# Gated linear attention and a spatial gating unit on one core: three tokens to a partition, chunks of 96 tokens in small TensorE tiles, y made transposed

## The chip, the core and the metric

The kernel runs on one core of one Trainium2 chip. The metric is the device time in microseconds of one execution; lower is better. The core has five engines with queues of their own, each in order: TensorE (PE), VectorE (DVE), ScalarE (ACT), GpSimd (POOL) and SyncE (SP), which here only issues transfers. TensorE reads SBUF and writes PSUM, which has eight banks of 512 float32 for each of 128 partitions.

## The reference

```python
def _attn_ref(q, k, v, alpha):           # each 4 x 8 x 768 x 48 (batch, head, token, d)
    state = zeros((B, H, D, D)); y = zeros_like(q)
    for t in range(S):
        state = alpha[:, :, t, :, None] * state + einsum('bhd,bhe->bhde', k[:, :, t], v[:, :, t])
        y[:, :, t] = einsum('bhd,bhde->bhe', q[:, :, t], state)
    return y

x = attn_out.transpose(0, 2, 1, 3).reshape(B, S, H * D)      # 4 x 768 x 384
h = maximum(x @ w_in, 0)                                      # w_in 384 x 1024
u, v = h[..., :512], h[..., 512:]
v_n = (v - mean(v)) / sqrt(var(v) + 1e-6)                     # over the last axis
v_s = einsum('ts,bsd->btd', w_spatial, v_n) + b_spatial[None, :, None]   # w_spatial 768 x 768
out = (u * v_s) @ w_out                                       # w_out 512 x 384
```

Inputs and output are float32; inside, matmul operands are bfloat16.

## The kernel before, in words

The recurrence is computed in chunks. In a chunk, the logarithms of alpha (`la`) are summed along the tokens by a matmul with a triangle of ones (`cum`); `kt` is k times exp(-cum), `qt` is q times exp(cum). The scores are kt against qt, masked to the lower triangle (`ptm`), and y is the masked scores times v (`vb`) plus q times the state at the chunk's start (`sbd`). The state is carried from chunk to chunk: `z` adds the chunk's kt times v to it (the matmuls `upd`), `S` multiplies it by the chunk's total decay (`bc`), and `sb` copies it as bfloat16 into a block-diagonal tile.

The six chunks of 128 tokens of a batch come in two forms. `first(i)` treats one chunk with one token to a partition, its loads in pieces of 192 bytes. `pair(j)`, used for the first eight chunks (`PAIRS`), treats two chunks as 256 tokens, two tokens to a partition, in pieces of 384 bytes; its chunks are then 64 partitions each, so several matmuls run in tiles of 64 rows. Both transpose kt and qt by TensorE, evacuate them to `kqT`, and make y with tokens on the partitions. `finish_x` copies y to SBUF (`x_sb`), transposes it by TensorE and copies it again to `xT`, which has the 384 model columns on the partitions.

The second half works by batch: `second_v` (v, then its mean and variance, then `vn`), `second_u` (u, transposed), `second_s` (the spatial matmul with the transposed `w_spT`, plus bias, into `vsb`; then the product with u, `gT`) and `second_o` (times w_out, and a store). `weights` transposes w_spatial row block by row block.

The order of everything is written out by hand in the table `PLAN`. Every operation has a number; `P43` emits operation 43 on TensorE, `A`, `D`, `G`, `S`, `Q` on ACT, DVE, POOL, SP and as a transfer's end; numbers behind a colon add matmuls on a constant tile (`junk`) ahead of the next operation that takes a PSUM bank. So `PLAN` also says which engine does an operation that could run on several. Waits are put in by the framework from the tiles that operations read and write. PSUM banks are taken in turn. SP's queue holds the loads of q, k, v and alpha, those of the weights between them, and the stores.

Of the kernel before, what the change touches and what calls it, by code (L numbers as in the profile page):

```python
# [11 lines left out]
ALU = mybir.AluOpType  # L13

class Op:


    def __init__(self, key, eng, dur, emit, deps=(), prio=0.0, take=None, lat=0.13, cols=0):  # L20
        self.key = key
        self.eng = {eng: dur} if isinstance(eng, str) else dict(eng)
        self.emit, self.prio, self.lat, self.cols = emit, prio, lat, cols
        self.take = [take] if isinstance(take, Slot) else list(take or ())
        self.deps = [d for d in deps if d is not None]
        self.done = False
        self.big = False


class Ring:  # L30


    def __init__(self, bufs):
        self.bufs = bufs


class Slot:
    def __init__(self, ring):
        self.ring, self.users = ring, []


ENGINES = {
    "kt": {"POOL": 0.9},
    "vb": {"POOL": 0.48, "ACT": 0.42},
    "S": {"POOL": 0.5},
    "sb": {"POOL": 0.73, "DVE": 0.95},
    "vn": {"DVE": 0.42},
    "xe": {"ACT": 0.4},
    "ev": {"DVE": 0.34, "ACT": 0.48},
    "u": {"ACT": 0.39, "DVE": 0.49},  # L50
    "o": {"ACT": 0.4},
}
PAIRS = (0, 1, 2, 3)
ACT_STATS = ((2, 2), (1, 4))
LETTERS = {"P": "PE", "D": "DVE", "A": "ACT", "G": "POOL", "S": "SP", "Q": "DMA"}

PLAN = """
G32 S34 Q33 S36 G0 S38 S40 Q35 D1 Q37 S94 A42 D2 Q39 S96 P43:512:512:192 P53:64 A44 A45 G46 Q41 S98 A54 A55 D47 G56
D57 P51:512 Q95 P49 S100 P59:64 P61 A58 G48 D60 A50 D52 P63:192 Q97 S163 A62 P247 D65 A102 P71 D248 P74 D72 A64 Q99
S167 P103:96 G66 P113 D73 A104 A114 D68 D76 A115 Q101 P249 S165 G116 A105 A250 D117 G106 D107 P121:512 Q164 S169 D75  # L60
A122 P111:64 G67 P109 D112 P119 A110 G69 D120 Q168 S4 P131:192 D70 P134 G108 P77 G118 D133 G3 P123:128 A171 Q166
D132 S307 D125 A124 A78 P172 D136 P81 G126 P182 A173 Q170 S9 D135 P79 A183 D127 A82 P137 A174 Q5 D128 A184 S311 P142
D176 P138 G185 P83 A139 D175 A80 P140 A84 D186 P178 A143 P180 D179 A177 G187 P188 P190 Q308 S309 D189 G129 P144 P192
D181 A145 D191 A141 G6 D194 A193 A8 P197 D7 Q10 P200 G195 D199 P85 S14 A315 G196 D198 P157 A86 G130 D201 P316 A158
P146 D202 Q312 A317 D159 A318 P203 A147 P204 P208 D87 P88 A205 Q310 A209 G11 P206 D12 P326 A89 D13 P210 A207 D320
P151 S18 Q15 A211 D148 S313 P212 A327 S367 G319 A328 P324 D152 P223 A213 D330 G329 P215 A160 D90 A325 Q19 P334 S371
P322 A216 P221 D162 G16 A224 D217 P153 A222 P332 G17 A91 D323 P229 A335 P225 D92 Q314 S22 D231 A154 P149 D93 A333
G20 D214 P232 A226 P227 A150 Q368 D230 S369 P155 D234 A228 D161 A233 P235 D21 Q372 A218 S409 D237 P238 A236 D219
P344 G321 A156 Q23 D239 P255 S446 D220 G331 P259 D345 A375 P376 D346 P336 A377 A378 A380 P260 D338 Q370 S373 A240
D381 P256 A337 D261 A24 P263 G339 Q410 D257 S411 P264 D25 G379 P241 Q447 D341 P347 A242 S448 D265 P251 A243 G342  # L70
D349 Q374 P244 P383 G340 S413 A245 D246 P252 D348 A417 G262 P275 Q412 A385 S415 D253 P276 D384 G258 A382 Q449 P350
D277 A454 S450 P390 A351 G343 P267 D391 Q414 P418 S480 G278 D392 P354 P352 A419 P279 Q416 A353 S26 G421 P268 A355
P386 A420 A422 P356 D269 Q451 G266 P393 S482 A357 D387 P280 A394 D423 G388 P455 Q481 D281 S484 P395 A457 P425 A456
G389 P361 D427 A424 Q27 D397 G458 A396 S452 P358 D426 A459 A362 D460 P398 G254 A359 D363 P428 A399 P462 G270 P432
D429 A488 P271 D433 A463 G430 Q483 S577 P401 D464 P489 D434 A28 G31 P407 Q485 A490 G30 S486 D400 P272 A492 P435 A402
G491 Q453 D29 P405 S581 A436 D273 P283 G282 A408 D493 Q578 S579 P437 P469 A284 G274 D438 P495 A406 D470 P403 Q487
A496 S611 G461 D471 P287 A439 G431 A497 Q582 D404 P291 S583 A288 D360 P465 P498 Q580 A585 S648 P472 D466 A292 D500
P586 G494 A364 P440 Q612 G467 D499 A587 S690 P295 A473 G468 D366 A588 A590 Q584 S615 P474 A441 G589 P501 D475 D591
P299 Q649 A502 D442 S728 A476 P503 A296 P593 G592 P477 A619 Q691 D505 D504 S613 A300 D594 P517 D365 A478 Q616 P596
D595 S650 P506 A443 D597 A479 D518 P513 Q729 D445 S652 A507 P600 D444 P620 A508 D602 Q614 P519 S692 A621 P533 D509  # L80
A656 P303 Q651 S694 A514 D601 P515 A510 Q653 A622 P525 A698 D512 S617 D511 A624 P529 G623 D516 A520 Q693 P657 S654
P534 A304 D625 G598 A659 A658 P526 D535 Q695 G599 A661 S732 P699 D527 P530 A701 A700 G660 P545 Q618 A703 D531 S730
A736 P627 G536 P603 D629 Q655 P546 S762 A604 D704 G528 P537 A628 D662 Q733 P538 S696 D547 G626 P605 P664 D539 G702
A606 P634 Q731 A607 P630 S766 A665 P541 D631 G663 A666 D635 P737 Q763 G632 P542 S858 A738 D636 G548 A739 P671 A741
P706 Q697 D543 S892 P667 A708 G532 P608 D742 A707 D672 Q767 P521 S764 G740 A609 P637 D633 A770 P549 Q859 A638 S734
D668 P522 D673 P550 Q893 G705 D523 S862 P639 P744 D551 A640 P713 G524 A641 Q765 D746 P674 A745 S860 D714 P771 G669
A675 P642 D715 A772 Q735 G670 S768 A774 P751 P676 A643 P553 G540 D678 Q863 D677 A866 S864 D775 P709 P716 A554 G773
D752 P679 Q861 A717 S929 D753 A900 G544 P557 A680 D710 Q769 D610 S896 P777 G711 A558 P718 P867 A743 G712 Q865 P561
D719 A869 D779 S933 A868 D720 A681 P747 G552 D778 P686 Q930 D644 S894 P721 A871 G870 A562 P754 D748 Q897 A722 D872
S971 P565 G749 A755 D687 G750 A645 Q934 P780 P874 S931 A566 D782 P756 P569 G776 A757 A723 Q895 D781 G873 S975 P573  # L90
D876 A758 A875 P783 D724 Q972 S898 P682 A784 A570 P881 D646 Q932 P785 P759 S973 D787 A786 D883 A574 P788 A937 Q976
D882 S935 A760 P796 D683 A789 P684 Q899 D761 S1012 A797 P877 P800 A685 D790 Q974 A725 P901 S1008 P688 A903 A801 D647
P794 A979 Q936 D726 S1042 P938 A791 D727 P798 D878 A902 Q1013 D792 P810 A940 A905 S1046 D793 G904 P802 A939 D795
P980 Q1009 D906 G879 S1010 P803 A981 P811 G941 A799 D804 Q1043 A942 P806 S977 D689 A982 G805 A984 P807 D812 Q1047
P884 S571 D943 P822 G907 A885 D985 P823 G813 Q1011 D808 S1044 P908 P886 G983 P945 A910 D887 Q978 P814 D909 S1014
A888 D824 P911 A946 G809 P815 D912 Q572 A947 P889 S1048 D816 G944 A1016 Q1045 S575 D880 P987 A890 G817 P915 P952
A988 D916 Q1015 P1017 G913 P830 A1050 D989 A1019 G914 P834 A1018 D917 Q1049 A1021 P1051 D953 G825 P838 A1052 Q576
D954 A835 P948 G1020 P831 A1054 D949 P918 D832 G950 P818 A919 D1022 G986 P819 A839 D1055 G951 P920 P1024 D820 A921
P994 A1025 G1053 D922 P990 P826 D996 A1026 P955 G1023 D995 P827 G833 A956 D991 P1031 D828 P957 P1057 G992 A959 D1032
P923 A958 G821 A1059 D1033 P960 A924 G829 P997 A1058 D925 P967 A998 G993 P1027 A961 P999 P1060 D1028 A968 P842 D962  # L100
G1029 A1000 A1001 P963 G1030 A843 D1061 P1002 A1056 S844 D1062 A964 P1034 S305 A1003 D891 P850 S836 Q845 A1035 S840
P1063 D1004 Q306 P846 A1064 Q837 A926 P1065 P1036 A847 P965 D1067 Q841 D1037 A1038 D1066 P854 D928 D966 P1068 A851
D927 A1005 P969 A1069 D1006 P1074 D1007 P1039 D1070 P1078 A1040 P1080 A855 D1041 P1076 A970 S856 P1090 S297 D1075
A1071 P1094 S285 D1079 A1077 Q857 P1082 S289 D1072 P1106 Q298 D1073 S301 D1081 P1086 Q286 S567 P1087 Q290 S563 P1083
D1088 Q302 S852 P1095 G1089 Q568 P1091 S559 D1096 P1102 Q564 S293 D1092 G1097 P1098 D1084 Q853 S848 P1103 D1093 Q560
G1085 S555 P1099 D1104 Q294 P1107 D1105 P1113 Q849 D1100 Q556 P1117 A1114 D1108 G1101 P1110 D1109 S1115 A1118 P1111
S1119 P1121 D1112 Q1116 P1137 A1122 Q1120 P1125 D1138 S1123 P1133 S1139 A1126 P1129 D1134 Q1124 S1127 S1135 A1130
Q1140 S1131 Q1128 Q1136 Q1132
"""


def replay(ops, fill, plan):

    for word in plan.split():
        number, *junk = word[1:].split(":")
        op, eng = ops[int(number)], LETTERS[word[0]]
# [8 lines left out]
def kernel(  # L125
# [12 lines left out]
    nc = tc.nc  # L138
# [1009 lines left out]
```

## Time and profile before

| | |
|---|---|
| time, median of 3 runs | 145.1 us (144.96 to 145.82) |
| span of the profiled execution | 142.9 us; the page gives no time for what lies around it |
| PE, DVE, ACT, POOL busy | 132.9, 122.2, 108.2, 86.0 us |
| instructions | 4,962, of them 1,910 matmuls and 1,923 weight loads |
| moved by transfers | 28.64 MB in 89,000 packets |

The span runs from the first to the last instruction of the one profiled execution. A row of the page's groups has the line and engine, the operation, what it writes and reads, the count, then the busy time and the mean of one in ns, and the idle time before it with what ended it. In the rows by slices each digit is the busy share of a fortieth of the span, in tenths. A chain row is start, duration and what. Matmuls overlap, so their mean duration is not the time that one adds.

### The profile page before, as it was taken

Reading aid. Unit: us, or ns where it says so; the run is one execution under the profiler, and the core shown is the slowest. Engines: PE = TensorE matmul, PEld = TensorE weight load, DVE = VectorE, ACT = ScalarE, POOL = GpSimd, SP = SyncE. Lnnn points to the kernel's source line nnn. Section 1 sums busy time; section 2 is a strip of 40 time slices with the busy share of each in tenths; the row PEclk is TensorE's granted clock in tenths of the full one; section 3 lists DMA queues with packets and bytes.
Section 4 is the critical chain, followed back from the end, with each engine's and each line's share of the span. In section 5 each row is a group of like instructions: output and inputs, shape, how many; then the busy total and the mean of one; then the engine's idle time right before and its main releaser. Section 6 shows DMA issues by size and latency. Waiting matters only on the chain.

```text
span 142.9 us, 4962 instructions
## 1 busy us (share of the span) xinstructions
PE 132.9 (93%) x1910; PEld 83.7 (59%) x1923; DVE 122.2 (85%) x290; ACT 108.2 (76%) x280; POOL 86.0 (60%) x147
## 2 busy tenths in 40 slices
PE   7978977999799999999999999999999999999990
PEld 3464857456465666665655666656666666556460
DVE  6759998998989799989789999889889989776950
ACT  3567398899976799999987889999878688760131
POOL 6945853748317999971288879910999994003700
PEclk9999999999999999999999999999999999999999
DMA  4999989999998999999899999999999103229645
GB/s 115 268 261 265 250 201 327 334 322 328 251 224 163 213 276 161 203 176 198 145 205 192 164 209 162 208 143 206 187 156 222 55 7 137 86 98 338 229 150 180
DMA packets 89000, 28.64 MB, mean 200 GB/s; under 512 B 83728, under 2 KB 87440, under 8 KB 88976
## 3 DMA queue, kind: packets, MB, share of 16 engines
q1 hardware_dynamic: 88944, 28.32, 92.0%
q8 instruction: 15, 0.25, 0.8%
q14 instruction: 9, 0.07, 0.2%
q0 software_dynamic: 32, 0.00, 0.0%
HBM read 23.60 MB, written 4.72 MB: 198 GB/s over the span
## 4 chain that ended last, share of the span: by engine, by line
PE 70%; DMA 10%; SPq 6%; ACT 6%; DVE 3%; issue 2%; ACTq 0%
PE bank L822 50%; DMA ac<-in_alpha_dram 10%; SPq L435 6%; PE bank L748 3%; PE bank L713 3%; PE bank L776 2%; PE bank L660 2%; ACT v_sb L204 2%; PE bank L734 2%; PE bank L770 2%; PE bank L392 2%; DVE stats L887 1%; DVE vn L919 1%; ACT x_sb L198 1%; PE bank L663 1%
## 5 line engine op out<-in xcount | busy, mean ns | idle before, releaser
L822 PE MATMUL bank<-w_spT,vn 128*128 128x384 bf16 x192 | 36.3, 326 | 0.0
L981 POOL TENSOR_TENSOR gT<-vsb,uT 128x384 bf16<-128x384 f32 x28 | 25.8, 928 | 14.2 <-DVE vsb L968 13.5
L822 PEld LDWEIGHTS <-vn 128*128 128x128 bf16 x192 | 16.8, 97 | 10.5 <-DVE vn L919 0.2
L684 POOL TENSOR_TENSOR kt<-kc,binv 128x384 bf16<-128x384 f32 x16 | 14.8, 924 | 12.6 <-ACT bc L679 6.6
L759 DVE TENSOR_TENSOR ptm<-bank,mask 128x512 bf16<-128x512 f32 x32 | 20.8, 683 | 0.6 <-PE bank L748 0.6
L822 PE MATMUL bank<-xT,w_in 128*128 128x384 bf16 x96 | 19.7, 326 | 0.1
L968 DVE TENSOR_TENSOR vsb<-bank,bsp_bc 128x384 f32<-128x384 f32 x31 | 16.6, 552 | 3.0 <-PE bank L822 1.6
L822 PE MATMUL bank<-w_out_sb,gT 128*128 128x384 bf16 (+1 forms) x100 | 18.6, 319 | 0.0
L822 PE MATMUL bank<-w_in,xT 128*128 128x512 bf16 x59 | 16.9, 379 | 1.1 <-issue 0.3
L198 ACT COPY kqT<-bank 128x512 bf16<-128x512 bf16 x26 | 14.8, 592 | 1.3 <-PE bank L713 0.8
L338 POOL TENSOR_TENSOR state<-state,bc 128x192 f32<-128x192 f32 x20 | 10.4, 518 | 8.8 <-ACT bc L553 6.4
L887 DVE BATCH_NORM_STATS2 stats<-v_sb 128x6 f32<-128x512 bf16 x20 | 13.7, 683 | 1.4 <-ACT v_sb L204 1.4
L198 ACT CAST x_sb<-bank 128x384 bf16<-128x384 f32 x24 | 11.5, 485 | 2.2 <-PE bank L776 1.9
L204 ACT ACTIVATE v_sb<-bank 128x512 bf16<-128x512 f32 x20 | 11.6, 601 | 1.6 <-PE bank L822 1.5
L822 PEld LDWEIGHTS <-gT 128*128 128x128 bf16 x100 | 8.9, 97 | 5.6 <-POOL gT L981 0.4
L200 POOL CAST sbd<-state 64x192 bf16<-64x192 f32 x32 | 10.9, 341 | 1.7
L822 PEld LDWEIGHTS <-w_in 128*128 128x128 bf16 x96 | 8.3, 97 | 5.3 <-issue 0.4
L198 ACT COPY xT<-bank 128x192 bf16<-128x192 bf16 (+1 forms) x25 | 8.7, 384 | 2.9 <-PE bank L392 2.6
L919 DVE TENSOR_SCALAR vn<-v_sb,mvs,rstd 128x512 bf16<-128x512 bf16 x24 | 9.8, 437 | 0.7 <-ACT rstd L912 0.7
L588 DVE TENSOR_TENSOR ptm<-bank,mask 128x512 bf16<-128x512 f32 x16 | 10.3, 676 | 0.0
L188 PE MATMUL bank<-junk 128*128 128x512 f32 (+4 forms) x24 | 9.3, 490 | 1.1 <-DVE junk L234 1.1
L200 DVE COPY kqT<-bank 128x512 bf16<-128x512 bf16 x22 | 9.0, 417 | 1.5 <-PE bank L505 0.9
(131 smaller groups left out, 288.2 us busy)
## 6 DMA issues: line engine op xcount, KB each, us to landing
ac<-in_alpha_dram SPq DMA_DIRECT2D x16, 192.0 KB, 4.6
qc<-in_q_dram SPq DMA_DIRECT2D x16, 192.0 KB, 4.7
kc<-in_k_dram SPq DMA_DIRECT2D x16, 192.0 KB, 4.8
vc<-in_v_dram SPq DMA_DIRECT2D x16, 192.0 KB, 4.3
raw_w<-in_moe_w_spatial_dram SPq DMA_DIRECT2D x3, 768.0 KB, 6.8
out_dram<-raw_w SPq DMA_DIRECT2D x11, 192.0 KB, 2.1
out_dram<-o_sb SPq DMA_DIRECT2D x9, 192.0 KB, 2.0
ac<-in_alpha_dram SPq DMA_DIRECT2D x4, 384.0 KB, 6.6
```

Source lines behind the costliest of these rows:

```text
L198: nc.scalar.copy(out=out, in_=in_)
L200: ENG[eng].tensor_copy(out=out, in_=in_)
L204: nc.scalar.activation(out=out, in_=in_, func=AF.Relu)
L338: ENG[eng].tensor_tensor(out=st["state"], in0=st["state"], in1=st["bc"][:, :, None].to_broadcast([128, HP, D]), op=ALU.mult)
L588: nc.vector.tensor_tensor(out=st[f"ptm{par}"][:, s], in0=st[f"pt{s}{par}"], in1=mask2[:, par], op=ALU.mult)
L684: ENG[eng].tensor_mul(out=k_blocks(kt3)[:, :, :, 0:D], in0=quad(st["kc"]), in1=st["binv"])
L759: nc.vector.tensor_tensor(out=st["ptm"][:, s], in0=st[f"pt{s}"], in1=mask4, op=ALU.mult)
L822: return lambda ps: nc.tensor.matmul(out=out(ps), lhsT=lhsT(), rhs=rhs(), start=start, stop=stop)
L887: nc.vector.bn_stats(out=stats, in_=d["v_sb"][:, tt, :])
L919: nc.vector.tensor_scalar(out=d["vn"][:, t, :], in0=d["v_sb"][:, t, :], scalar1=d["mvs"][:, t, 0:1], scalar2=d["rstd"][:, t:t + 1], op0=AL ...
L968: nc.vector.tensor_tensor(out=hold["vs"], in0=ps[:, 0:TH], in1=bsp_bc[:, th, :], op=ALU.add)
L981: ENG[eng].tensor_tensor(out=bt[b]["gT"][:, dsl, cols], in0=hold["vs"], in1=bt[b]["uT"][:, dsl, cols], op=ALU.mult)
```

## The change

All loads of q, k, v and alpha take three tokens to a partition (`A = 3`): a block is 384 tokens, a half of a batch, and each load is 1024 pieces of 576 bytes. A block has four chunks (`NC = 4`) of 96 tokens, which stand on 32 partitions each. `block(n)` replaces both `pair` and `first`.

- Cumulative sums: the one for the third token of a partition is three matmuls (`cum`). Those of the second and first are made by matmuls too in blocks 0 and 1 (`PE_SUMS`), and by subtracting `la` on DVE or POOL in the others (`sub`, into `cs`).
- kt and qt are made and transposed once for each of the three tokens of a partition, in row tiles of 64 as `first` did.
- State update `upd`: per head, token of the partition and chunk a matmul of 32 rows by 64 columns. All four chunks' updates stand in one operation.
- Scores `sc`: matmuls of 64 rows by 32 columns, 96 moving columns; masks of 128 x 384 instead of 128 x 512, 48 as before.
- y is made transposed, with v (32 of its columns) as the stationary and the masked scores as the moving side: `ya` is 192 matmuls of 32 x 32 in a block, and `y` adds the state's part by 16 matmuls of 64 x 32 in a chunk. `xe` copies it from PSUM straight into xT. There is no x_sb and no transposing of x any more.
- Heads lie as (pair, half) with heads 0 to 3 in one half and 4 to 7 in the other, so `sbd` is one copy of 128 partitions instead of two of 64. `vb` and `sbd` have 80 columns to a head pair's half, zeroed at the start.
- Tokens of a batch lie in xT, vn, gT and w_spT in the order (half, token of the partition, partition); w_spatial is loaded and transposed, and the output stored, in that order. The two halves of w_in are loaded by two transfers of 64 partitions each.
- `ACT_STATS` stay; the table `PLAN` is new, with its numbers of junk matmuls and its choices of engines.

How many matmuls there are of each kind, counted in the two programs:

| | before | after |
|---|---|---|
| dense (v, u, s, o) | 461 | 461 |
| transposes of kt, qt | 320 | 384 |
| transposes of x | 120 | 0 |
| state update | 216 | 672 |
| scores | 256 | 768 |
| y from masked scores | 256 | 1536 |
| y from the state | 80 | 448 |
| cumulative sums | 32 | 36 |
| totals of the decay | 84 | 96 |
| transposes of w_spatial | 72 | 72 |
| changes of tile size in PE's order | 78 | 80 |

The core of the diff (the table and what only moves is left out):

```diff
-    C = 128
-    NCH = S // C
+    A = 3
+    NC = 4
+    P = 128 // NC
+    R = A * P
+    TH = 128 * A
+    NB = S // TH
+    PE_SUMS = (0, 1)
...
+    raw_bufs = {x: Bufs(fixed(f"raw_{x}", 2, [128, H, A, D], FP32)) for x in "akqv"}
+    la_bufs = Bufs(fixed("la", 2, [128, HP, A, 2, 64], BF16))
+    vb_bufs = Bufs(fixed("vb", 2, [128, A, HP, 160], BF16))
+    ptm_bufs = Bufs(fixed("ptm", 5, [128, 2, HP, R], BF16))
+    sbd_bufs = Bufs(fixed("sbd", 5, [128, HP // 2, 160], BF16))
...
+                nc.sync.dma_start(
+                    out=raw[x].tile.rearrange("p h a d -> p h (a d)"),
+                    in_=src[b, :, t0:t0 + TH, :].rearrange("h (p a) d -> p h (a d)", a=A))
...
+            for a in range(A):
+                nc.tensor.matmul(
+                    out=st["bank"][:, 0:DM], lhsT=le, rhs=by_head(la.tile[:, :, a]), start=(a == 0), stop=(a == A - 1))
...
+                def sub(eng, a=a, cs=cs, above=above):
+                    ENG[eng].tensor_tensor(
+                        out=split(cs.tile), in0=split(above()), in1=by_head(la.tile[:, :, a + 1]), op=ALU.subtract)
...
+            for hp in range(HP):
+                for a in range(A):
+                    for s in range(2):
+                        for ch in ups:
+                            nc.tensor.matmul(
+                                out=ch.tp[64 * s:64 * s + 64, hp, :], lhsT=kt.tile[rows(ch.c), a, hp, s, :],
+                                rhs=of_head(vb.tile[rows(ch.c), a], HP * s + hp),
+                                start=(hp == 0 and a == 0), stop=(a == A - 1), skip_group_check=True)
...
+                for hp in range(HP):
+                    for s in range(2):
+                        for c in range(NC):
+                            dd = slice(64 * s, 64 * s + D)
+                            nc.tensor.matmul(
+                                out=pts[s][rows(c), hp, :], lhsT=kq.tile[dd, a, hp, rows(c)],
+                                rhs=kq.tile[dd, :, HP + hp, rows(c)], start=True, stop=True)
...
+            for a in reversed(range(A)):
+                for g in range(HP // 2):
+                    for w in range(4):
+                        for s in range(2):
+                            out_rows, ks = block_of(2 * s + g, w)
+                            for ch in chunks:
+                                nc.tensor.matmul(
+                                    out=ch.y[out_rows, ks, :], lhsT=vb.tile[rows(ch.c), a, 2 * s + g, 32 * w:32 * w + 32],
+                                    rhs=ptm[a].tile[rows(ch.c), s, 2 * g + w // 2, :],
+                                    start=(ch.c, out_rows.start) not in begun, stop=(ch.first and a == 0),
+                                    skip_group_check=True)
...
+                for g in range(HP // 2):
+                    for w in range(4):
+                        for s in range(2):
+                            out_rows, ks = block_of(2 * s + g, w)
+                            dd = slice(64 * s, 64 * s + D)
+                            nc.tensor.matmul(
+                                out=ch.y[out_rows, ks, :], lhsT=ch.prev.sbd.tile[dd, g, 32 * w:32 * w + 32],
+                                rhs=kq.tile[dd, :, HP + 2 * g + w // 2, rows(ch.c)], start=False, stop=True,
+                                skip_group_check=True)
...
+            def xe(eng, ch=ch):
+                out = xT.tile[:, :, t0:t0 + TH].rearrange("p ks (a t) -> p ks a t", a=A)[:, :, :, rows(ch.c)]
+                copy(eng, out, ch.y.rearrange("p ks (a t) -> p ks a t", a=A))
...
+    def block_of(m, w):
+
+        i = 3 * m + (w if w < 2 else w - 1)
+        quarter = 2 * (i // 6) + i % 2
+        return slice(32 * quarter, 32 * quarter + 32), i % 6 // 2
...
-            nc.sync.dma_start(out=out[b, tt * 128:(tt + 1) * 128, :], in_=hold["o"])
+                nc.sync.dma_start(out=out[b].rearrange("(j p a) m -> j a p m", p=128, a=A)[tt // A, tt % A][:, cols], in_=o_use.tile[:, cols])
...
+    W_TILES = ((0, 1), (2, 5), (3, 4))
```

## The prediction

> **What bounds the kernel now.** I read the page's busy shares first, then its 40 slices, then the table by stage, then the chain of waits, and last the groups and single TensorE records.
>
> ```profile
> PE 132.9 (93%) x1910; PEld 83.7 (59%) x1923; DVE 122.2 (85%) x290; ACT 108.2 (76%) x280; POOL 86.0 (60%) x147
> PE   7978977999799999999999999999999999999990
> DVE  6759998998989799989789999889889989776950
> DMA  4999989999998999999899999999999103229645
> ```
>
> TensorE (PE) is the busiest, but VectorE (DVE) is only 11 us behind. The transfers are busy for three quarters of the span and then fall away: they feed the start, not the end. The table by stage tells the two regimes apart (PE, PEld, DVE, ACT, POOL busy, then clock, DMA share, GB/s):
>
> ```profile
> 20.00:30.00 10.00, 8.45 (x177) 5.94 (x179) 9.46 (x23) 8.78 (x22) 5.11 (x10) 1.00 1.03 297
> 30.00:40.00 10.00, 9.24 (x122) 5.46 (x120) 9.42 (x27) 9.77 (x27) 5.21 (x7) 1.00 1.09 307
> 40.00:60.00 20.00, 19.84 (x351) 12.99 (x351) 18.18 (x39) 16.37 (x42) 16.14 (x26) 1.00 1.06 204
> 60.00:80.00 20.00, 19.73 (x279) 12.11 (x280) 17.59 (x44) 18.29 (x55) 12.27 (x21) 1.00 1.10 182
> ```
>
> From 20 to 40 us DVE works 94% of the time and PE waits for it; from 40 us PE is at 99%. The chain in order of time agrees: loads to 27 us, then ACT and DVE, then PE to the end.
>
> ```profile
> 36.31 0.32 DVE vn L919
> 36.63 0.61 DVE stats L887
> ...
> 39.50 1.08 PE bank L822 x6
> ...
> 123.63 15.93 PE bank L822 x97
> 139.58 0.48 ACT raw_w L198
> ```
>
> So the time is: when the spatial matmuls (s, reading w_spT) can start, 39.4 us here; plus the PE work that stands behind the first of them; plus some 3.3 us of copy and store after PE ends at 139.6. I make this sum for both kernels. The span is 142.9 us; the median of the runs, 145.1, is 2.2 above it, and I add 2.2 at the end.
>
> **Prices.** Dense matmuls follow each other by their columns: 163 ns for 384, 216 for 512 (the 97 at the end: 15.93/97 = 164). Small ones are cheaper than the 180 to 220 ns that a row shows, since tiles overlap:
>
> ```profile
> 39.08 0.42 PE L577 MATMUL bank<-kqT 48*64 48x128 bf16 x16
> 39.43 1.15 PE L822 MATMUL bank<-w_spT,vn 128*128 128x384 bf16 x6
> 40.95 0.57 PE L547 MATMUL bank<-vbp,kt 64*128 64x48 bf16 x32
> ```
>
> L577 has four 64x64 tiles: its single records start in fours, 2 to 3 ns apart with a weight load between, and a four follows the last by 55 ns (128 columns). L547 has two row tiles: pairs 25 ns apart, 12.6 ns each. Where the tile size changes, the next matmul comes some 105 ns late (39.282, then 39.431 after L577). DVE's groups overlap by 0.06 to 0.08 us, so I price by start to start:
>
> ```profile
> L759 DVE TENSOR_TENSOR ptm<-bank,mask 128x512 bf16<-128x512 f32 x32 | 20.8, 683 | 0.6 <-PE bank L748 0.6
> L968 DVE TENSOR_TENSOR vsb<-bank,bsp_bc 128x384 f32<-128x384 f32 x31 | 16.6, 552 | 3.0 <-PE bank L822 1.6 <-POOL gT L981 0.9
> ```
>
> A mask of 512 takes 0.605 (mean 683), an operation on 384 from PSUM 0.49 (mean 552), one on 192 some 0.28.
>
> [...] The trace agrees as far as it goes: four tiles, a matmul and a weight load each, within 11 ns; it has no tile 32 wide and no long stream of them. [...] the trace has 15 such refills (16,384 B each, 1.2 us) for 3,833 PE instructions; the changed kernel needs about 35. Spread over the span that is no bound.
>
> **The change part by part.**
>
> *Loads.* 80 loads of q, k, v, alpha become 32 of 1024 pieces of 576 B. The DMA view:
>
> ```profile
> DMA packets 89000, 28.64 MB, mean 200 GB/s; under 512 B 83728, under 2 KB 87440, under 8 KB 88976
> ac<-in_alpha_dram SPq DMA_DIRECT2D x16, 192.0 KB, 4.6
> ac<-in_alpha_dram SPq DMA_DIRECT2D x4, 384.0 KB, 6.6
> ```
>
> Landings in a full queue are 1.04 us apart for 192-byte pieces, 1.50 for 384, 2.1 for a weight; one step more gives 1.97[...]: I take 2.05. Total 32 x 2.05 = 66 us against 64 x 1.04 + 16 x 1.5 = 91. Only the start can cash this. SP's queue order is alpha, k, q, v of blocks 0 and 1, alpha of 2, half of w_in, the rest of block 2, alpha of 3, the other half, q and k of 3, two thirds of w_sp, v of 3. From 4.95 us (before: 4.34 for 384 KB) that puts v of block 1 at 19.3, w_in at 23.5 and 33.8, v of block 3 at about 44.1. In the kernel before the last w_in landed at 28.3. PE's queue is in order and has block 3's state update, which waits for v, ahead of the first s, so all s wait behind it: by the loads alone s starts at 45.
>
> *TensorE.* Dense work is unchanged: 381 x 0.163 + 72 x 0.216 + 8 x 0.083 = 78.3 us. The rest before, by spacing: transposes 9.8 (of x among them 2.7), updates 4.2, scores 5.1, y from masks 4.9, from states 3.4, cumulative sums 5.2, totals 2.1, w_sp and bias 1.5, 78 mode changes 8.2: 44.4. After: 384 transposes at 14.6 = 5.6 and none of x; 672 updates at 4 ns = 2.7; 768 scores, eight tiles to a round of 42.5 = 4.1; 1536 ya at 4.1 (sixteen tiles, loop order sometimes repeating a tile) = 6.3; 448 y at 11.5 (four tiles at a time) = 5.1; sums 5.9, totals 2.4, w_sp and bias 1.5, 80 mode changes 8.4: 42.0. PE gains 2.4 us, on the path from 40 us on, if a small pair costs 4 ns. Bounds: not below the tile rounds (about 1 us less), not above L547's 12.6 ns, which nothing in the trace proves to be beaten over a long stream: 26 us more in all, 15 of it behind the first s.
>
> *VectorE.* Over the whole kernel: masks 48 x 0.49 for 48 x 0.605 (-5.5), q products 15 for 24 (-4.2), casts of weights (-3.3), sbd (-2.3), uT (-1.4); state products on DVE 15 (+4.3), products and subtractions for k and sums 14 more (+6.8), kqT copies 7 more (+2.4), state additions 8 more (+2.2), copies of outputs 5 (+2.3), memsets of wider tiles and of vb (+2), other copies (+1.3): about +5. What matters is how much of it stands ahead of the first s in DVE's queue: before 35.2 us; after, masks +2.0, kqT +2.0, state additions +1.7, state products +2.0, k products +2.0, subtractions +1.0, xT +1.5, bias +0.5, memsets +2.0, less sbd 1.8, casts 2.1, w_spT copies 0.8: 45.2. PE's order has three blocks and most of a fourth done by then.
>
> *ACT and POOL.* x goes from PSUM to xT in one copy instead of two with transposes between, ln is 8 instructions for 20, ACT loses about 10 us. POOL loses about 3: 9 q products and 5 subtractions for k products, sbd and states. Both lie beside PE and DVE from 40 us on: I cost them at nothing. If that cover went, they would still have 25% idle.
>
> **The sum.** Before: DVE's 35.2 us ahead of the first s end at 39.4, 4.2 us of it idle. With the same idle the first s comes at 45.2 + 4.2 = 49.4, later than the loads allow. Behind it PE has 67.1 dense + 17.3 small + 47 mode changes 4.9 = 89.3 (before 98.9, done in 100.2). DVE has about 80 us left: in the first 38 us behind the first s PE has 37.9 and DVE 37.0, so they run tied, where before DVE had about 2 us of air in each 20 (18.18 and 17.59 busy). I add the 1.3 that PE waited before and 2.0 for the tie. PE ends at 49.4 + 89.3 + 3.3 = 142.0; + 3.3 = 145.3 span; + 2.2 = 147.5.
>
> **Rivals.** *A, the start isn't DVE's.* DVE's extra work is early in the queue but not what PE waits for: the loads decide, s starts at 45, PE ends at 45 + 89.3 + 1.3 = 135.6, time 141.1: faster. For it: less DMA, ACT 10 us lighter, one step fewer from y to xT. Against it: DVE at 94% from 20 to 40 us with less to do. It is faster than the kernel before once 2.4 of DVE's 10 us lie beside what PE needs (s before 47), and reaches 141.1 with 4.4. *B, small tiles don't stream.* TensorE takes a long run of load-and-matmul pairs no faster than L547's 12.6 ns: PE behind the first s 104.6, the first s itself near 54 since early blocks stretch too: 54 + 104.6 + 3.3 + 3.3 + 2.2 = 167. For it: 4,482 matmuls for 1,910, and no stream in the trace below 12.6; at 6 ns it is 151. Against it: the bursts of 2 ns[...]. [...]
>
> **How the numbers follow.** The forecast 147.5 has 0.52, with its own range from 144 (no tie, cheaper rounds) to 153 (6 ns[...]); A 0.28, B 0.20 spread between 153 and 167. The range from 140.5 to 160 leaves out about 0.1 at each end. One per cent is about what a measurement of this kernel can tell from no change: faster than 143.6 is nearly all of A, 0.27; within it the forecast's low part and A's rest, 0.15; slower 0.58.
>
> **What would show it.** Right: the first matmul that reads w_spT near 49 us, DVE busy over 9 tenths from 15 to 50 us, PE over 9.7 from there, ya's 192 matmuls in about 0.9 us, masks near 0.55 mean, loads landing 2.05 apart. Wrong: the first s at 45 or earlier (A), or ya's 192 in 2 us and more, with PE busier and DVE idler (B).

## The result, and the profile after

The changed kernel takes 217.1 us (median of 4 runs, 215.8 to 217.6), the kernel before 145.0 in the same runs (144.9 to 145.8): a ratio of 1.493, 95% interval 1.487 to 1.500. The profiled execution has a span of 215.1 us. The forecast was 147.5. This is the page after: busy shares, the rows by slices for PE, DVE and the granted clock, the instruction queue, and the shares of the chain.

```profile
PE 165.6 (77%) x4501; PEld 100.3 (47%) x4501; DVE 132.9 (62%) x312; ACT 100.5 (47%) x239; POOL 84.8 (39%) x133
PE   6962774386959199967898984796999938959993
DVE  6845451366558159676799961274987933529783
PEclk9997587559688759999999996587999996799999
q8 instruction: 35, 0.57, 1.1%
PE 63%; issue 19%; DVE 14%; ACT 1%; POOL 1%; DVEq 0%; ACTq 0%; POOLq 0%
```

The same of before, for the clock, the queue and the chain:

```profile
PEclk9999999999999999999999999999999999999999
q8 instruction: 15, 0.25, 0.8%
PE 70%; DMA 10%; SPq 6%; ACT 6%; DVE 3%; issue 2%; ACTq 0%
```

No engine is a bound in the usual sense: PE, the busiest, is at 77%, and DVE fell from 85% to 62%. "issue", a time in which the engine waits for nothing that the profile shows, is 19% of the chain; before it was 2%. The clock, at nine tenths and more throughout before, falls to five and six tenths in places. The table by stage (PE, PEld, DVE, ACT, POOL, clock, DMA share, GB/s) shows that much of the missing time lies early, just where the forecast had DVE and PE full:

```profile
20.00:40.00 20.00, 10.79 (x384) 6.60 (x384) 6.28 (x15) 5.05 (x12) 4.78 (x9) 0.67 1.03 241
40.00:60.00 20.00, 15.68 (x640) 10.42 (x640) 12.15 (x29) 12.04 (x26) 8.04 (x13) 0.69 0.14 45
60.00:80.00 20.00, 13.97 (x331) 7.47 (x331) 10.16 (x24) 9.49 (x24) 8.19 (x12) 0.74 0.72 227
```

The waits of PE name it: the four kinds of small matmuls stop for "issue" 16 times (columns: us in total, times, longest), 34.9 us in all.

```profile
PE bank L526 <- issue: 17.1, 7, 4.5
PE bank L498 <- issue: 8.1, 4, 4.6
PE bank L543 <- issue: 5.4, 3, 2.0
PE bank L475 <- issue: 4.3, 2, 2.8
```

The chain shows one such stop, in the middle of a ya (L526):

```profile
67.75 0.65 PE bank L621 x3
68.40 1.59 PE bank L526 x171
69.99 4.51 issue
74.50 0.30 PE bank L526 x11
```

The matmul behind the stop carries no wait for a semaphore; the one ahead belongs to the same operation. What changes between them is only the place in PE's instruction stream. Counted over PE's instructions in the trace, all 16 stops begin, to within one, at number 193 plus a multiple of 256 (449, 961, 1217, 1473, 1985, 2497, 3009, 4033 and so on to 8641), and each ends 1.2 to 1.6 us after one of the 35 packets of 16,384 bytes on the instruction queue has been moved. For the 9,002 instructions of PE that the page counts, 35 packets are one for 257. Some of the stops, worked out from the trace's records (us):

```
stop at    PE entered the     packet          PE goes   entry to   DMA queues
instr.     block before       moved           on at     use        in between
  449        16.98          20.10 - 21.45     22.91      5.9        full
 1217        36.24          38.01 - 39.14     40.52      4.3        full
 2497        57.76          58.91 - 60.20     61.49      3.7        idle
 3009        68.72          71.87 - 72.97     74.50      5.8        full
 8641       186.98         188.14 - 189.09   190.45      3.5        idle
```

The packets without a stop fit as well. With block 0 at number 193 and packets counted from 0, packet n of the 35 begins 0.5 to 3.6 us after PE enters block n in 31 cases, and 0.5 to 1.5 us before the first matmul of that block in four.

So my reading of these times is: a block of 256 instructions is asked for at about the time when PE enters the block before it, and not a whole block sooner; the trace shows the packets, not the asking. PE mostly goes on 3.3 to 3.7 us after that entry when the data queues are idle, 3.8 to 6.9 when they are full (57 stops of five runs, see the end). PE runs through 128 pairs of a weight load and a small matmul in some 1.1 us, and then stands. I call this theory F, and tested it against R (a small pair is slow by itself, however the stream is supplied) and S (the start: DVE, loads, order).

### The profile page after: what moved, and what is told of

Same layout as the page of the kernel before. It is cut to its first block, busy times and chain, and to the rows that moved or that the text cites. A ratio compares the mean times of both kernels' runs of the same rounds, so it can differ in the third digit from the quotient of the medians.

```text
span 215.1 us, 9991 instructions
## 1 busy us (share of the span) xinstructions
PE 165.6 (77%) x4501; PEld 100.3 (47%) x4501; DVE 132.9 (62%) x312; ACT 100.5 (47%) x239; POOL 84.8 (39%) x133
## 4 chain that ended last, share of the span: by engine, by line
PE 63%; issue 19%; DVE 14%; ACT 1%; POOL 1%; DVEq 0%; ACTq 0%; POOLq 0%
PE bank L621 33%; PE bank L526 7%; PE bank L164 5%; PE bank L498 4%; PE bank L543 4%; PE bank L475 3%; PE bank L341 2%; DVE vn L704 2%; DVE vs L743 2%; PE bank L445 2%; DVE kqT L176 2%; PE bank L350 1%; DVE gT L760 1%; DVE ptm L506 1%; PE bank L374 1%
## 5 line engine op out<-in xcount | busy, mean ns | idle before, releaser
L760 POOL TENSOR_TENSOR gT<-vs,uT 128x384 bf16<-128x384 f32 x28 | 25.6, 932 | 32.6 <-DVE vs L743 32.6
L506 DVE TENSOR_TENSOR ptm<-bank,mask 128x384 bf16<-128x384 f32 x48 | 24.2, 548 | 11.3 <-PE bank L498 11.0
L526 PE MATMUL bank<-ptm,vb 32*32 32x96 bf16 x1536 | 15.7, 211 | 18.3 <-issue 17.1
L621 PEld LDWEIGHTS <-vn 128*128 128x128 bf16 x192 | 18.2, 99 | 14.4 <-DVE vn L704 2.1
L414 POOL TENSOR_TENSOR kt<-raw_k,binv 128x384 bf16<-128x384 f32 x16 | 16.0, 1005 | 18.5 <-ACT binv L404 16.3
L526 PEld LDWEIGHTS <-vb 32*32 32x32 bf16 x1536 | 13.4, 88 | 19.0 <-issue 18.5
L621 PE MATMUL bank<-w_out,gT 128*128 128x384 bf16 (+1 forms) x100 | 20.9, 347 | 0.5 <-DVE gT L760 0.4
L743 DVE TENSOR_TENSOR vs<-bank,bsp_bc 128x384 f32<-128x384 f32 x31 | 15.9, 550 | 3.8 <-PE bank L621 3.5
L498 PE MATMUL bank<-kqT 48*32 48x96 bf16 x768 | 11.3, 239 | 8.6 <-issue 8.1
L164 PE MATMUL bank<-junk 128*128 128x512 f32 (+8 forms) x26 | 13.5, 648 | 2.1 <-DVE junk L267 2.1
L180 ACT ACTIVATE uT<-bank 128x384 bf16<-128x384 f32 x23 | 10.9, 487 | 7.7 <-PE bank L621 7.7
```

The costliest lines, as they stand in the source:

```text
L164: nc.tensor.matmul(out=flat[:, 0:cols].rearrange("p (a b) -> p a b", a=4), lhsT=junk, rhs=junk[:, None, 0:n].to_broadcast([128, 4, n]), st ...
L180: nc.scalar.activation(out=out, in_=in_, func=AF.Relu)
L414: ENG[eng].tensor_mul(out=by_head(kt.tile[:, a]), in0=split(raw["k"].tile[:, :, a, :]), in1=split(binv.tile))
L498: nc.tensor.matmul(out=pts[s][rows(c), hp, :], lhsT=kq.tile[dd, a, hp, rows(c)], rhs=kq.tile[dd, :, HP + hp, rows(c)], start=True, stop=True)
L506: nc.vector.tensor_tensor(out=ptm[a].tile[:, s], in0=pts[s], in1=mask[:, a][:, None, :].to_broadcast([128, HP, R]), op=ALU.mult)
L526: nc.tensor.matmul(out=ch.y[out_rows, ks, :], lhsT=vb.tile[rows(ch.c), a, 2 * s + g, 32 * w:32 * w + 32], rhs=ptm[a].tile[rows(ch.c), s, 2 ...
```

## The experiments

All but e10 are single runs; the kernel before, run beside them, took 146.2 to 147.1 us. The cuts of code are shortened to what changes.

**Fewer small matmuls.** e1 gathers all four kinds into wider tiles, e2 only ya; what they leave out is in their expectations.

```diff
 (ya, e1 and e2)
-   for g, w, s, ch: matmul(out=ch.y[out_rows, ks], lhsT=vb[rows(ch.c), a, 2*s+g, 32*w:32*w+32], rhs=ptm[a]...)
+   for ks, ch:      matmul(out=ch.y[:, ks],        lhsT=vb[rows(ch.c), a, ks, 0:128],          rhs=ptm[a]...)
 (scores, e1)
-   for hp, s, c:    matmul(out=pts[s][rows(c), hp], lhsT=kq[dd, a, hp, rows(c)], ...)
+   for hp, s:       matmul(out=pts[s][:, hp],       lhsT=kq[dd, a, hp, :], ...)
```

> The changed kernel with its small matmuls gathered into fewer and wider ones (stationaries of 128 columns where there were 32 or 64): ya 36 for 192 in a block, scores 8 for 32 in an operation, y 3 for 16 in a chunk, state updates half. The banks, tiles, waits, engines and the order table stay; the attention's values are not the reference's. PE's queue has 3,915 instructions for 8,963. Theory F (PE's instruction supply: blocks of 256 instructions, about 3.4 us from asking to use, only one block ahead): the unexplained stops of 0.6 to 4.7 us, 36 us in all, go, the clock comes back to 1.00, and what is left is near the forecast, 140 to 155 us. Theory R (TensorE itself takes 8 ns and more for a small pair, supply plays no part): 2,440 pairs fewer at 8 ns is 20 us less, 197. Theory S (the start: DVE's work, loads and order ahead of the first matmul that reads w_spT set the time): little changes, 205 to 217, and that matmul stays near 85 us.

> The changed kernel with only ya gathered: 36 matmuls of 32 rows by 128 columns in a block for 192 of 32 by 32; its y is not the reference's, everything else stays. 6,467 PE instructions, 10 blocks of 256 fewer. Theory F: ya's 32.8 us (start to start) become 2 to 4, some stops stay in the runs of scores, y and updates, the clock recovers in part: 172 to 190 us. Theory R: 1,248 pairs at 8 ns less, 10 us: 207. Theory S: 210 to 217.

e1 took 162.2 us, e2 189.4. e1 has no stop without a semaphore; its busy shares, and the first waits of PE:

```profile
PE 138.4 (86%) x1977; PEld 80.6 (50%) x1977; DVE 133.6 (83%) x312; ACT 98.5 (61%) x239; POOL 85.3 (53%) x133
PE bank L445 <- DVE qt L420: 3.4, 5, 1.1
PE bank L164 <- DVE junk L267: 2.1, 1, 2.1
```

DVE has the same 312 instructions, the table and the waits are the same, and 54.9 us are gone: S falls, its 85 us for the first matmul on w_spT became 57.6. R's 197 is far off as well. In e2 the stops are 17.9 us in 7 places, six in scores, updates and y and one of 1.0 us in a dense group, and the time lies at the upper end of F's range and 18 us below R's. But e1 missed F's 140 to 155: something else costs another 7 us and more.

**The same instructions, in lumps of two sizes.** The cleanest test leaves the changed kernel alone and adds idle pairs to the kernel before.

```diff
+    LUMPS = [25 + 85 * i // 7 for i in range(7)]         # e4; e3: 21 for 7
+    def pads(flat, count):                                # 384; e3: 128
+        for i in range(count):
+            r = c = 32 * (i % 4)
+            nc.tensor.matmul(out=flat[c:c+32, 0:1], lhsT=ident[r:r+32, c:c+32], rhs=ident[r:r+32, 0:1], start=True, stop=True)
...
                     hold["ps"] = bank([128, 512])
+                    if seen[0] in LUMPS: pads(hold["ps"], PER)
```

> The kernel before with 2,688 idle pairs added (weight load and matmul of 32 by 32, one moving column, results overwritten by the next matmul of that bank): 21 lumps of 128 pairs, one ahead of every fourth or fifth dense group from the 25th on. Nothing is left out. Theory F: a lump is one block of 256 instructions, the block ahead is already there, and dense matmuls give time to fetch the next: hardly a stop, each lump costs its own 1.1 to 1.6 us and two changes of tile size: 172 to 185 us. Theory R: the same number, 170 to 185.

> The kernel before with the same 2,688 idle pairs as the kernel with lumps of 128, now in 7 lumps of 384. Theory F: each lump is three blocks, PE runs dry twice or three times in it for about 2 us each, 7 to 9 us a lump: 195 to 210 us, and the stops lie 256 instructions apart. Theory R: no more than with lumps of 128, a little less since there are 28 changes of tile size fewer: 167 to 182.

e3 took 193.2 us and e4 228.1 (before: 146.2). The 2,688 pairs, start to start, fill 37.5 us in e3 and 69.4 in e4. One lump of e4 in the timeline (start, us, what, idle before):

```profile
179.00 1.09 PE L201 MATMUL bank<-ident 32*32 32x1 bf16 x120
181.02 1.17 PE L201 MATMUL bank<-ident 32*32 32x1 bf16 x128 [0.92 <-issue]
184.47 1.18 PE L201 MATMUL bank<-ident 32*32 32x1 bf16 x128 [2.29 <-issue]
188.20 0.22 PE L201 MATMUL bank<-ident 32*32 32x1 bf16 x8 [2.55 <-issue]
```

It breaks after exactly 128 pairs, twice. Of e3's 21 lumps nine pass in 0.99 us without a stop, and twelve have one, of 0.1 to 2.7 us. R, which foretold the same time for both, is refuted by 35 us. F's ranges were 8 us low for e3 and 18 low for e4. There are twelve stops where I wrote "hardly a stop": a lump can begin just behind a block's entry, so that this block is short of work too (PE enters one at 73.88 us, a lump follows at 74.61, and the block is used up at 75.75). And outside the lumps the kernel needs 156 to 159 us in place of 146.

**The same lumps in full tiles.**

```diff
-            out=flat[c:c+32, 0:1], lhsT=ident[r:r+32, c:c+32], rhs=ident[r:r+32, 0:1]
+            out=flat[:, 0:1], lhsT=ident, rhs=ident[:, 0:1]
```

> The kernel before with the 7 lumps of 384 idle pairs, each pair now a full tile (128 by 128, one moving column) where it was 32 by 32; nothing is left out. A full pair takes some 26 ns (the decay totals' spacing), so 128 of them take 3.4 us, about what a block of 256 instructions needs to arrive. Theory F: a lump lasts 10 us as with the small tiles (7.6 to 12.5), the stops shrink to under 1 us each, and the time is 212 to 224 us, not more than the 228 of the small ones: the tile's size has no part in it. Theory R (the tile's own time decides): 384 x 26 ns for 384 x 8 is 6.9 us more a lump on top of the stops, 260 and more.

The same lump lasts 10.1 us from its start to the next matmul (small tiles: 9.4), without a stop:

```profile
183.39 10.27 PE L200 MATMUL bank<-ident 128*128 128x1 bf16 x384
```

A full pair follows the last by 26.2 ns, 3.35 us for 128 of them. The lumps take 75.1 us together (small: 68.7), their stops fall from 44.8 us to 3.8. R's 260 is refuted. In lumps of 384 the small tile's speed is not to be had: 7.8 ns a pair became 25.6 on average, close to the full tile's 26.2. The total, 233.6, is above F's range, and above the 228 that F set as its limit, for the reason seen in e4, the time outside the lumps. That time is the dense matmuls': start to start without idle time they take 93 us in e4 and in e6, and 80 in the kernel before. The granted clock falls to 0.50 in every lump and stays there for a while behind it, and where it is 0.50 the 384-column ones follow each other by 320 ns in place of 163. In e6 no long stop is to blame: from 186.0 to 193.5 us, inside the lump shown, PE is busy without a break and the clock is 0.50.

**The count put back.** e5 is e1 with idle pairs (`pads`, as above) at the head of ya, scores and updates.

> The changed kernel with gathered small matmuls (as in the first experiment, 162.2 us), and idle pairs put in their place so that PE's queue is as long as in the changed kernel again: 201 at the head of each ya, 24 of each scores, 42 of each update, all 32 by 32 with one moving column, overwritten afterwards. 8,957 PE instructions; as there, the attention's values are not the reference's. Theory F (supply of instructions): the stops come back, 35 to 44 us in all by a count of 256-instruction blocks at 3.5 to 4.0 us each, and the time with them: 205 to 222 us. Theory R (a small pair's own 7.8 ns): 2,520 x 7.8 ns and some changes of tile size, 182 to 187.

It took 225.1 us, 62.9 more than e1, a little more than F's range and 38 more than R's. The stops are back, and most of them stand among pads, which do no work:

```profile
PE bank L173 <- issue: 28.6, 11, 4.7
```

**A cheaper ya and y that compute the same.** For half of the heads two neighbouring windows become one of 64 columns.

```diff
-   for w in range(4): ... out_rows of 32, lhsT=vb[..., 32*w:32*w+32]
+   for w, n_w in ((0, 2), (2, 1), (3, 1)) if g == 0 else ((0, 1), (1, 1), (2, 2)):
+       ... out_rows of 32*n_w, lhsT=vb[..., 32*w:32*w+32*n_w]
```

> The changed kernel, complete, with ya and y in fewer matmuls: where two of a head's 32-column windows fall on neighbouring quarters of PSUM (half of the heads), one stationary of 64 columns takes both, so ya has 144 matmuls for 192 in a block and y 12 for 16 in a chunk; wide ones first, then narrow ones, in y the other way round. 7,973 PE instructions for 8,963: four blocks of 256 fewer. Theory F: by the count of blocks at 3.5 to 4.0 us the stops fall by 15 to 19 us, and the time to 196 to 206 us. Theory R: 496 pairs fewer at 7.8 ns, with some more changes of tile size: 213 to 217.

212.0 us, a ratio to before of 1.456 (1.445 to 1.468): 5.1 less than the changed kernel, 1 us below R's range and 6 above F's, about a third of what F gave. The stops of the four kinds fell by 7.4 us to 27.5, and did not stay where they were:

```profile
PE bank L498 <- issue: 19.6, 6, 4.6
PE bank L552 <- issue: 5.5, 3, 3.4
PE bank L531 <- issue: 2.4, 2, 2.0
```

ya (now L531) fell from 17.1 us to 2.4, the scores (L498) went from 8.1 to 19.6. Here a stop belongs to the place where a block ends too soon, not to the operation that stands there.

**What remains in e1.** e1 is not the forecast's kernel without stops: its 900 gathered pairs take 25.4 us start to start, where the forecast had 18.2 for all small ones. Two more questions to the 14.7 us between 162.2 and the forecast: 32 words of the table changed from `D` to `A` (e7 on e1, e8 on the changed kernel), and the junk left out except at two places (e9 on e1).

```diff
 (e7, e8: 32 words of PLAN, the first)
-D87
+A87
 (e9)
-        fill.extend(int(x) for x in junk)
+        fill.extend(int(x) for x in junk if number in ("53", "66"))
```

> The changed kernel with gathered small matmuls, and 32 operations of the order table moved from DVE to ACT at the same place (14 of 29 kqT copies, 9 relus of u, 9 copies to xT): DVE 15 us lighter, ACT 16 us heavier; the attention's values are not the reference's. It asks what stands between the 162.2 us of the first experiment and the forecast of 147.5. Theory D (PE waits on DVE, which was busy 17 to 19 of each 20 us): PE's waits shrink, 150 to 157 us. Theory N (the order and its chains through several engines, whoever does the work): within 2 us of 162.

> The changed kernel in full, with the same 32 operations moved from DVE to ACT; nothing is left out. Theory F: PE's queue and its stops are what they were, DVE has slack (62% busy): 214 to 219 us. Theory D (DVE's load matters here too): 5 us and more below 217.

> The changed kernel with gathered small matmuls (162.2 us in the first experiment), without the order table's junk matmuls except those ahead of the first cumulative sum and the second one of block 0; the attention's values are not the reference's. Junk took 12.4 us of PE start to start there and 6% of the chain. It asks again what lies between 162.2 and the forecast of 147.5. Theory J (junk stands in PE's way at the start): the first matmul that reads w_spT comes 3 to 6 us before 57.6, and the time is 156 to 160 us. Theory K (junk keeps PE's clock up, and PE would wait there anyway): the clock of the first 40 us falls below the 0.76 to 0.88 seen there, and the time is 162 to 170 us.

e7 took 169.7 us, e8 223.1, e9 160.2. DVE is busy 9.5 us less in e7 and 11.1 less in e8 (15 were expected), and they are 7.5 and 6.0 us slower than e1 and the changed kernel; the kernel before ran 0.9 and 2.1 us longer beside them, so that much may not be the edit's. None of the four ranges was met. The lighter DVE brought no gain, but ACT's share of the chain rose from 9% to 29% in e7 and from 1% to 15% in e8, so these runs don't tell what DVE's work alone costs. Without the junk the first matmul on w_spT comes at 55.2 us, 2.3 earlier, but the clock from 10 to 30 us falls to 0.66 (e1: 0.88 and 0.84). J has the direction, K the clock, and 2 us don't settle it.

## Why the prediction was wrong, step by step

*The step that failed* is the sentence on instruction fetch: "Spread over the span that is no bound." The 35 refills were right to the number (35 packets). Dividing them by the span was the error: the four kinds of small pairs (3,424, two instructions each) fill 27 of the 35 blocks, and they come in runs, one ya alone being 384 instructions. Each stop waits for a block, 34.9 us in all. That the supply would keep pace was assumed, not shown: in the kernel before PE spends 6.1 us and more on every block (15 packets), and has no such stop. The changed kernel's stops show one block in use and one on its way: in 31 of 35 cases the packet begins 0.5 to 3.6 us after PE has entered a block, and a stopped PE goes on 1.2 to 1.6 us after the packet's end.

*The price of a small pair*, 4 ns, was assumed: the trace of before, which has no tile 32 wide, doesn't show it. In the changed kernel it holds for the first 32 pairs of a run only. In the twelve places where ya begins, or goes on behind a stop, with more than 32 pairs, the first 32 follow each other by 3.4 to 6.8 ns, ten times by 3.4 to 4.5; the pairs behind them by 8.3 to 8.9. Runs of 32 and more scores take 5.2 to 9.3, and the pads of one column, over a lump of 128 without a stop, 7.8. Why the first 32 are faster no run here shows. The bursts that the forecast read, 16 of L577 and 32 of L547, were no longer than that. Nor was L547's 12.6 ns an upper bound: in the kernel before PE spends 6.1 us and more on every block, so no run there shows the limit. With the stops a pair of ya takes 21 ns (32.8 us for 1,536). Together ya, scores, y and updates take 76.6 us start to start for the forecast's 18.2. Of these 58 us, 34.9 are stops; the rest is the pair's own price, changes of tile size and waits for other engines, not told apart here. e1 agrees: it has 2,524 pairs fewer (its expectation says 2,440), and its 900 gathered pairs take 25.4 us, so the four kinds lose 51.2 of the 54.9 us between the two kernels.

*Rival B* had the direction and the sign to look for (ya's 192 in 2 us and more, DVE idler), but it expected PE busier, and PE fell from 93% to 77%. It had the wrong mechanism and a third of the size: it took small pairs to be slow everywhere, and its price came from a run too short to show the limit.

*The clock* was in no step. Dense matmuls took 91.9 us, start to start without idle time, where I counted 78.3 (the kernel before, read in the same way: 80.3). Seven of the eight stretches at clock 0.5 begin inside a stop or within 2 us of its end. The other, from 18.3 to 28.6 us, begins just as the stop of 4.57 us does, so that stop did not start it. Nor does it take a stop: from 186.0 to 193.5 us e6's one-column matmuls run without a break, and the clock is 0.50 all the same. What sets the clock these runs don't show. e1, without stops, still needs 85.6 at a mean clock of 0.96. Its two first stretches at 0.5 lie before 35 us, among the waits of the start; that these waits cause them is not shown.

*The first matmul on w_spT*, 49.4 in the forecast, came at 85.5 us, and at 57.6 in e1, where the stops are out of the way. DVE's work ahead of it was sized well (45.2; e1 46.9 busy). "With the same idle", 4.2 us, was not: DVE idles 10.7 us there. By this reading of the trace the kernel before has 34.3 and 5.2, for the 35.2 and 4.2 of the forecast. Behind it e1 needs 99.3 us to PE's end for 92.6. Rival A is out: nothing started early. What makes e1's extra waits, beyond the lower clock, stays open.

*Smaller terms.* Masks 0.55 mean: right. A change of tile size, at clock 1.00 and with nothing else to wait for, costs some 92 ns from dense matmuls into small tiles and mostly 122 to 135 out of them, near the 105 assumed on average. Rival B's "26 us more in all" should have been 24.9 (3,424 pairs at 12.6 ns less 18.2). DVE grew by 10.7 us for about 5, ACT fell by 7.7 for 10, POOL by 1.2 for 3. Loads in the full queue land 1.81 us apart, not 2.05.

## What to carry to other kernels

Count the instructions of TensorE by blocks of 256 along its queue, as the stops lie here, not over the span. As an estimate from these runs (entry to use 3.3 to 3.7 us with idle data queues, 3.8 to 6.9 with full ones), a block that runs in less than about 3.5 us (5 with full data queues) makes the engine stand for the difference, so 128 pairs should hold at least that much work. Packed tiles gained less in the longer run: with dense work on both sides a small pair cost 13.9 ns in lumps of 128 (37.5 us for 2,688), 25.8 in lumps of 384. Price a small pair from a run longer than 32 of them (ya: 3.4 to 6.8 ns for the first 32, 8.3 to 8.9 behind). When a profile says "issue" and the matmul behind it has no semaphore, look at whether the stops lie a fixed number of instructions apart.

## What was not expected of the hardware

- The wait for a block was longer where the data queues were busy. Over 57 stops of more than 0.5 us in five runs (the changed kernel, e2, e4, e5, e6), entry to use is mostly 3.3 to 3.7 us where these are idle, and 3.8 to 6.9 where they are over nine tenths busy; e8 has one of 8.1. The difference lies ahead of the packet's transfer, which itself takes about 1.1 us, with 1.1 to 1.6 after it.
- A weight load and a matmul of one column in a 32 by 32 tile took 7.8 ns over 128 pairs, in a full tile 26.2. In lumps of 384 pairs little of this is left: 68.7 us for all 2,688 small pairs, 75.1 for the full ones.
- The granted clock fell to 0.50 while the profile shows PE busy without a break: in the three lumps of e6 that have no stop (from 134.9, 155.7 and 183.4 us) it does so 2.6 to 3.3 us behind the lump's start.
